# Attention, routed experts and phase mixing on one core: the shared expert slot in four column groups of 32, and a later fifth chunk

## Chip, cores and metric

One core of one Trainium2 chip runs the whole program as a single launch. The metric is device time in microseconds (us). Three runs of the kernel before gave 809.20, 811.64 and 813.08 us; their median is 811.64. The profile is one more execution.

## The reference

Three stages on `B, S, D = 4, 576, 64` with 8 heads, so 2304 tokens of 512 numbers, all in 32-bit floats:

```python
# 1. attention: scores below (row maximum - tau) are masked
scores = scale * q @ k.T
scores = where(scores >= max(scores) - tau, scores, -1e9)
x = softmax(scores) @ v                       # heads side by side: (B, S, 512)
# 2. experts: each token picks one of 8, or keeps the expert of the token before it
fresh = argmax(x @ w_gate); keep = sigmoid(x @ w_local) >= 0.5
e = previous_e if keep else fresh             # along the sequence
x = softmax(x @ w_gate)[e] * (relu(x @ w1[e]) @ w2[e])     # 512 -> 1024 -> 512
# 3. phase mixing
theta = x @ w_theta
y = w_tok_r @ (x * cos(theta)) + w_tok_i @ (x * sin(theta))
u = x + y
out = u + relu(u @ w_ch)
```

Weights of the third stage are given as 64-bit floats and are decoded on the core.

## The kernel before

**Stages.** Attention runs first, batch by batch, and the router's work in between. It writes the tokens to memory and a list that sorts them by expert. The second stage works on that list in slots of 128 tokens (single) or 256 tokens of one expert (two). A slot gathers its tokens by an indirect DMA, loads its expert's two weight matrices, multiplies, scales by the gate and scatters the rows to `scr_m`. The third stage reads `scr_m` batch by batch.

**The shared slot.** The last slot of the second stage holds tokens of two experts: 96 of one and 32 of another ("few"). Here the products are in plain 32-bit floats, and each matmul takes two passes on TensorE. The tokens are the stationary operand, the weights stream through; a matmul of some columns (tokens) writes the partitions of those tokens. So `cols` has one entry for each group of tokens with its weight tiles: tokens 0 to 63 and 64 to 95 with the first expert's, 96 to 127 with few's. For each half `z` of the 1024 hidden numbers it runs four `k` steps over the 512 inputs, then the relu on ScalarE; `turn` transposes a half of `h` for the second matrix. Then come eight `k` steps over the 1024 hidden numbers, the scaling and the scatter. The first expert's w1 lies in `w1r` and `raw`, its w2 in `w2r`; few's lie in the two tiles `stk`, w1 in the one, w2 in the other.

**Channel words.** The last matrix of the third stage, `w_ch`, comes as pairs of 32-bit words and is decoded in eight pieces beside the last slots. `more_words` issues the loads of two pieces (`stage_words`, L1486) into a ring of two buffers, so a load waits until the piece before it in that buffer has been read. `decode(n)` takes n steps of the decoding: three bit operations and a product on DVE (L1520 to L1529), a square on GpSimd (L1521); the split of a decoded piece into a high part (ScalarE, L1512) and a low one (GpSimd, L1513) comes with the first steps of the pieces behind it, or, with none left, in steps of its own.

**Order.** In these stages the instructions of TensorE, ScalarE and DVE run in the order in which the program has them (`manual_schedule(engines=MANUAL)`). SP, which issues the loads, and GpSimd are not in that list in this slot: their order is a scheduler's, with the program's order as a preference. Each engine's queue is served in order.

**Into the third stage.** `load_first_x` loads the first batch's rows, chunk by chunk of 128 tokens, before the shared slot's scatter: the slots still open have no tokens of the first batch. The fifth chunk has only 64 tokens of the first batch; its other half holds 64 tokens of the second batch, and its load (L1670) waits for the shared slot's scatter. `mix_all` (from L1560 on) is the third stage. `prep` transposes chunks (L1698), splits them in a high and a low part (L1699, L1700) and, for the chunks in `rest`, keeps a full copy (L1704). `theta(b, dh, g)` makes the angles of one half `dh` of the 512 columns for a group `g` of chunks: groups 0 and 1 have two chunks, 24 matmuls, group 2 has the fifth chunk, 12 matmuls. `wave_steps` turns angles into the products with cosine and sine: `tk` on ScalarE (L1738), four steps on DVE (L1740 to L1746), absolute value and two sines on ScalarE, products on DVE (L1752, L1754, L1761), the high parts (L1770) and the low parts `zl` and `zml` (L1779). The digits given to `wave` say which group takes its next step. `mix` (L1790 to L1792) is the token mixing: 27 matmuls a group, over all chunks, the fifth (`zmh`, `zml`) last.

The functions that the diff touches, with the line numbers of the profile:

Of the kernel before, what the change touches and what calls it, by code (L numbers as in the profile page):

```python
# [10 lines left out]
F32 = mybir.dt.float32  # L11
# [13 lines left out]
P = 128  # L25
# [7 lines left out]
SHARE = 96, 32  # L33
# [1 line left out]
STEPS = 1, 4  # L35
FAST = 117
WARM = 10
RING, SHARED_STEPS = 3, (4, 4, 10)
MANUAL = {mybir.EngineType.PE, mybir.EngineType.Activation, mybir.EngineType.DVE}
ORDERED = MANUAL | {mybir.EngineType.SP}  # L40
KH = S // 2 + D
# [13 lines left out]
class Kernel:  # L55
# [874 lines left out]
    def two_step(self, now, nxt, last, after):  # L930
        if after:
            self.load_index(after)
        few = nxt.get("few")
        for c in range(4):
            self.load_w1(nxt, c)
        if last:
            self.hidden_pair(now)
            self.hidden_out(last)
            self.pair_values(last, now)
            for _ in range(2):  # L940
                self.decode(STEPS[0] << self.halves)
        else:
            for f in range(4):
                self.hidden_two(now, f)
                if f < 3:
                    self.split_w2(now, f)
                self.decode(STEPS[0] << self.halves)
        self.more_words()
        for c in range(3):
            self.load_w2(nxt, c)  # L950
        self.tokens(nxt)
        for c in range(3):
            self.finish_two(now, c)
        if few:
            views = [[t[:, i * F:(i + 1) * F] for i in range(4)] for t in self.open_stk(F32)]
            few["w1raw"] = views[0]
            few["w2raw"] = [v.rearrange("p (t f) -> p t f", t=2) for v in views[1]]
            for c in range(4):
                self.load_w1(few, c)
        else:  # L960
            for c in range(2):
                self.split_w1(nxt, c)
        self.split_w2(now, 3)
        self.load_w2(nxt, 3)
        self.finish_two(now, 3)
        if few:
            for c in range(4):
                self.load_w2(few, c)
        else:
            for c in range(2, 4):  # L970
                self.split_w1(nxt, c)
        self.decode(STEPS[1] << self.halves)
        for h in range(2):
            self.scale(now, h, nxt["xt"][:, 1] if few else None)
            self.scatter(now, h)

    def shared_slot(self, st):
        nc = self.nc
        few, cols = st["few"], []
        for a, b, w in ((0, 64, st), (64, SHARE[0], st), (SHARE[0], P, few)):  # L980
            cols.append((slice(a, b), w.get("w1raw", self.w1raw), w.get("w2raw", self.w2raw)))
        self.more_words()
        h = self.hg.tile([P, F], F32, name="h")
        hf = self.xg.tile([P, 4, 2 * P], F32, name="xl").rearrange("p a b -> p (a b)")

        def turn(z):
            t = self.ps_x.tile([P, 4, P], F32, name="t").rearrange("p a b -> p (a b)")
            for i in range(4):
                nc.tensor.transpose(
                    t[:, i * P:(i + 1) * P], h[:, z * 512 + i * P:z * 512 + (i + 1) * P], self.ident)  # L990
            nc.scalar.activation(hf[:, z * 512:(z + 1) * 512], t, AF.Copy)
        for z in range(2):
            zs = slice(z * 512, (z + 1) * 512)
            hp = self.ps_h.tile([P, 2, 2 * P], F32, name="h").rearrange("p a b -> p (a b)")
            for k in range(4):
                for c, w1, _ in cols:
                    nc.tensor.matmul(
                        hp[c], st["xf"][:, k, c], w1[k][:, zs], start=(k == 0), stop=(k == 3), skip_group_check=True)
                if z and k == 1:
                    turn(0)  # L1000
            nc.scalar.activation(h[:, zs], hp, AF.Relu)
            self.decode(SHARED_STEPS[z])
        self.load_first_x()
        self.more_words()
        st["o"] = o = self.ps_o.tile([P, DM], F32, name="o")
        for k in range(8):
            for c, _, w2 in cols:
                nc.tensor.matmul(
                    o[c], hf[:, k * P:(k + 1) * P][:, c], w2[k // 2][:, k % 2], start=(k == 0), stop=(k == 7),
                    skip_group_check=True)  # L1010
            if k == 1:
                turn(1)
        self.decode(SHARED_STEPS[2])
        self.scale(st)
        self.scatter(st)

# [543 lines left out]
    def mix_all(self):  # L1560
# [6 lines left out]

        nc.scalar.activation(self.halfpi, self.ident[:, 0:1], AF.Sin)
        nc.vector.memset(self.halfpi, math.pi / 2)
        self.theta(0, 0, 0)  # L1570
        self.prep(0, (4,), (2,))
        for dh in range(2):
            for g in range(1 - dh, 3):
                self.theta(0, dh, g, self.ps_v if dh or g == 2 else self.ps_th)
        self.waves(0, 0)
        self.wave("01")
        self.prep(0, (), (3, 4))
        self.wave("0000" "21111" "00" "0" "2222" "11" "0" "1" "2" "1" "2" "2" "2")
        self.waves(0, 1)
        self.wave("012")  # L1580
        self.rest = []
# [108 lines left out]
    def prep(self, b, chunks, rest=()):  # L1690

        nc = self.nc
        st = self.state3[b]
        for c in chunks:
            cs = slice(c * P, (c + 1) * P)
            st["t", c] = t = self.ps_v.tile([P, 512], F32, name="v").rearrange("p (k s) -> p k s", k=4)
            for k in range(4):
                nc.tensor.transpose(t[:, k], st["x"][:, c, k * P:(k + 1) * P], self.ident)  # L1698
            nc.scalar.activation(st["xh"][:, :, cs], t, AF.Copy)  # L1699
            nc.vector.tensor_tensor(st["xl"][:, :, cs], t, st["xh"][:, :, cs].bitcast(F32), ALU.subtract)  # L1700
        for c in rest:
            n = self.chunk(c)
            for dh in range(2):
                nc.scalar.activation(  # L1704
                    st["xf", dh][:, :, c * P:c * P + n], st["t", c][:, 2 * dh:2 * dh + 2, :n], AF.Copy)
# [208 lines left out]
```

## Time and profile before

| what | value |
|---|---|
| median of three runs | 811.64 us (809.20 to 813.08) |
| the profiled execution: its time / its span | 809.36 us / 807.6 us |
| TensorE busy, weight loads busy | 773.2 us (96%), 614.3 us (76%) |
| DVE, ScalarE, GpSimd busy | 582.1 (72%), 471.9 (58%), 196.0 us (24%) |
| the shared slot's passes on TensorE | from 529.21 us on, scaled at 562.34 |
| mean DMA rate over the span | 132 GB/s |

The profile is that of one execution. Times in it count from the start of its span. PE is TensorE's matmuls, PEld its weight loads, DVE is VectorE, ACT ScalarE, POOL GpSimd, SPq the queue of DMAs that SP issues. `out<-in` are the program's names of tiles with numbers left out; L997 is a line of the kernel. A form like `128*32 128x512 f32` for a matmul is the part of the array it takes (rows by columns) and the streaming operand. An "x3" at the end of a row means that three neighbouring instructions of that line are merged in it; the duration is then from the first one's start to the last one's end. In brackets stands how long the engine was idle before, and what ended it. Matmuls are pipelined: what counts is the distance from start to start.

### The profile page before, as it was taken

The numbers are of one execution on the slowest core, as the hardware profiler recorded it, in microseconds if no ns is written. First come the engines' busy times: TensorE is split into PE (matmuls) and PEld (weight loads), VectorE is DVE, ScalarE is ACT, GpSimd is POOL, SyncE is SP. The second block draws the span as 40 slices with busy tenths as digits, with TensorE's granted clock in tenths as the row PEclk, the third lists the DMA queues.
The fourth block names the chain that finished last, engine by engine and source line by source line (L and its number), as shares of the span: only waits on it lengthen the run. The fifth ranks groups of instructions, "written<-read, shape, count | busy, mean of one in ns | idle before, by whom it ended". The sixth has DMA issues, their size and how long they took to land. (4 is left out here: it accounts for less than half of the span.)

```text
span 807.6 us, 16486 instructions
## 1 busy us (share of the span) xinstructions
PE 773.2 (96%) x6230; PEld 614.3 (76%) x6230; DVE 582.1 (72%) x1246; ACT 471.9 (58%) x941; POOL 196.0 (24%) x241
## 2 busy tenths in 40 slices
PE   7899999999999989999999999999899999999997
PEld 4455565565565578789999889932899999999997
DVE  6999999899989688568788889532695446555522
ACT  5998888887877745556555556412655335435311
POOL 4000003003002222136554455422002122033110
PEclk9999999999999999999999999999999999999999
DMA  6722323322411788789787776461010120120101
GB/s 153 183 75 81 90 75 101 115 75 76 119 48 61 261 278 213 258 329 316 262 281 244 253 241 224 159 234 54 11 53 1 46 80 1 41 72 2 59 1 59
DMA packets 67518, 106.70 MB, mean 132 GB/s; under 512 B 28194, under 2 KB 34726, under 8 KB 67432
## 3 DMA queue, kind: packets, MB, share of 16 engines
q1 hardware_dynamic: 63400, 95.33, 37.2%
q0 software_dynamic: 4032, 10.25, 3.5%
q8 instruction: 52, 0.85, 0.4%
q14 instruction: 34, 0.28, 0.1%
HBM read 94.22 MB, written 16.32 MB: 137 GB/s over the span
## 5 line engine op out<-in xcount | busy, mean ns | idle before, releaser
L332 DVE TENSOR_SCALAR_CACHE_REDUCE ns<-s,nqs 128x576 f32<-128x576 f32 x144 | 116.8, 812 | 18.6 <-PE s L313 16.6
L372 DVE SCALAR_TENSOR_TENSOR a<-ns,thr,e 128x576 f32<-128x576 f32 x144 | 117.1, 814 | 0.7 <-ACT thr L345 0.6
L338 ACT ACTIVATE e<-ns,nb 128x576 f32<-128x576 f32 x144 | 109.6, 781 | 10.3 <-DVE ns L332 10.3
L413 ACT ACTIVATE aT<-t 128x256 f32<-128x256 f32 (+1 forms) x216 | 82.6, 457 | 30.3 <-PE t L406 29.4
L313 PE MATMUL s<-raw 64*128 64x288 f32 x512 | 81.6, 427 | 9.1 <-ACT aT L399 5.0
L437 PE MATMUL o<-aT,vm 128*64 128x288 f32 x512 | 74.8, 415 | 0.0
L1304 PE MATMUL h<-xh,stk 128*128 128x256 f32 x256 | 72.9, 285 | 0.6 <-DVE hl L1293 0.6
L1305 PE MATMUL h<-xl,stk 128*128 128x256 f32 x256 | 72.4, 283 | 0.0
L1306 PE MATMUL h<-xh,stk 128*128 128x256 f32 x256 | 72.4, 283 | 0.0
L1418 DVE TENSOR_TENSOR w2l<-w2r,w2h 128x1024 fp32r<-128x1024 f32 x42 | 54.6, 1306 | 11.6 <-ACT w2h L1415 11.6
L313 PEld LDWEIGHTS s<-raw 64*128 64x128 f32 x512 | 43.5, 189 | 23.8 <-DVE ns L332 8.7
L1320 PE MATMUL o<-w2l,hh 128*128 128x512 f32 x144 | 56.4, 392 | 0.9 <-DVE w2l L1418 0.9
L437 PEld LDWEIGHTS o<-aT,vm 128*64 128x64 f32 x512 | 32.8, 136 | 32.1 <-issue 12.8
L1319 PE MATMUL o<-w2h,hh 128*128 128x512 f32 x144 | 56.9, 395 | 0.0
L1321 PE MATMUL o<-w2h,hl 128*128 128x512 f32 x144 | 56.2, 390 | 0.0
L406 PEld LDWEIGHTS t<-ident,a 64*128 64x128 f32 x1152 | 42.6, 139 | 15.4 <-ACT e L338 6.3
L406 PE MATMUL t<-ident,a 64*128 64x64 f32 x1152 | 51.6, 228 | 0.2 <-ACT aT L413 0.2
L1304 PEld LDWEIGHTS h<-xh,stk 128*128 128x128 f32 x256 | 49.1, 192 | 2.0 <-DVE hl L1293 1.7
L1415 ACT ACTIVATE w2h<-w2r 128x1024 fp32r<-128x1024 f32 x42 | 44.0, 1054 | 10.9 <-issue 7.9
L1292 ACT ACTIVATE hh<-h 128x512 fp32r<-128x512 f32 x36 | 21.3, 598 | 48.7 <-PE h L1306 43.3
L1305 PEld LDWEIGHTS h<-xl,stk 128*128 128x128 f32 x256 | 49.1, 192 | 0.5 <-issue 0.2
L1306 PEld LDWEIGHTS h<-xh,stk 128*128 128x128 f32 x256 | 49.1, 192 | 0.0
(387 smaller groups left out, 2069.2 us busy)
## 6 DMA issues: line engine op xcount, KB each, us to landing
w2r<-in_moe_w_dram SPq DMA_DIRECT2D x48, 512.0 KB, 6.5
raw<-in_moe_w_dram SPq DMA_DIRECT2D x36, 512.0 KB, 8.0
raw<-in_q_dram SPq DMA_DIRECT2D x15, 576.0 KB, 5.9
w1r<-in_moe_w_dram SPq DMA_DIRECT2D x12, 512.0 KB, 5.5
raw<-in_k_dram SPq DMA_DIRECT2D x30, 176.0 KB, 3.5
vm<-in_v_dram SPq DMA_DIRECT2D x32, 128.0 KB, 2.5
stk<-in_moe_w_dram SPq DMA_DIRECT2D x8, 512.0 KB, 7.1
out_dram<-ob SPq DMA_DIRECT2D x16, 256.0 KB, 2.2
```

Of the source, the lines that this page charges most:

```text
L313: nc.tensor.matmul(s[:, z, :SH], qd[rows, int(j != z), cs], kd[rows, j * KH:j * KH + SH], start=True, stop=True)
L332: nc.vector.tensor_scalar(ns, s[:, :, :SH], self.nqs[:, 0:1], None, ALU.mult, ALU.min, accum_out=nb)
L338: self.nc.scalar.activation(e, pr["s", c, j], AF.Exp, bias=pr["nb", c][:, j:j + 1], scale=-1.0)
L372: nc.vector.scalar_tensor_tensor(a.rearrange("p (z s) -> p z s", z=2), s, thr, e, ALU.is_le, ALU.mult, accum_out=total)
L406: nc.tensor.transpose(t[h][:, 4 * n + b], a[r, (k + b) * P:(k + b + 1) * P], self.ident[r, r])
L413: nc.scalar.activation(self.pairs[i]["aT"][:, b:b + w, s0:s0 + D], t[h][:, 4 * n:4 * n + w], AF.Copy)
L437: self.last_av = nc.tensor.matmul(o[j * D:(j + 1) * D, :SH], vm[:, j, c - 1, :], aT[:, 4 * j + c - 1, zs], start=(z == 0 and c == 1), stop ...
L1304: nc.tensor.matmul(h[:, i], wh[:, fs], xh, start=(k == 0), stop=False)
L1305: nc.tensor.matmul(h[:, i], wh[:, fs], xl, start=False, stop=False)
L1306: nc.tensor.matmul(h[:, i], wl[:, fs], xh, start=False, stop=(k == 3))
L1319: nc.tensor.matmul(o, hh, wh[:, i], start=(q == i == 0), stop=False)
L1320: nc.tensor.matmul(o, hh, wl[:, i], start=False, stop=False)
```

## The change

The shared slot's tokens are cut into four groups of 32, each with the weight tiles of its expert: three of the first expert and one of few. The loads of few's w2 move from the slot before into the shared slot, behind its first `more_words`. The decoding steps move ahead of each half's relu, eight in each half; the second `more_words` moves from behind `load_first_x` to behind the first half's relu, and after the second matrix the decoding runs until nothing is left. In the third stage the fifth chunk is transposed behind the first two groups of angles of the first half, and the first steps of their waves; the angles of that chunk come after the first group of the other half. The buffer of the fifth chunk's transposes is taken from its pool ahead of the others' angles.

```diff
--- before.py
+++ after.py
@@ -35,7 +35,7 @@
 STEPS = 1, 4
 FAST = 117
 WARM = 10
-RING, SHARED_STEPS = 3, (4, 4, 10)
+RING, SHARED_STEPS = 3, (8, 8)
 MANUAL = {mybir.EngineType.PE, mybir.EngineType.Activation, mybir.EngineType.DVE}
 ORDERED = MANUAL | {mybir.EngineType.SP}
 KH = S // 2 + D
@@ -963,10 +963,7 @@
         self.split_w2(now, 3)
         self.load_w2(nxt, 3)
         self.finish_two(now, 3)
-        if few:
-            for c in range(4):
-                self.load_w2(few, c)
-        else:
+        if not few:
             for c in range(2, 4):
                 self.split_w1(nxt, c)
         self.decode(STEPS[1] << self.halves)
@@ -977,9 +974,12 @@
     def shared_slot(self, st):
         nc = self.nc
         few, cols = st["few"], []
-        for a, b, w in ((0, 64, st), (64, SHARE[0], st), (SHARE[0], P, few)):
-            cols.append((slice(a, b), w.get("w1raw", self.w1raw), w.get("w2raw", self.w2raw)))
+        for a in range(0, P, 32):
+            w = st if a < SHARE[0] else few
+            cols.append((slice(a, a + 32), w.get("w1raw", self.w1raw), w.get("w2raw", self.w2raw)))
         self.more_words()
+        for c in range(4):
+            self.load_w2(few, c)
         h = self.hg.tile([P, F], F32, name="h")
         hf = self.xg.tile([P, 4, 2 * P], F32, name="xl").rearrange("p a b -> p (a b)")
 
@@ -998,10 +998,11 @@
                         hp[c], st["xf"][:, k, c], w1[k][:, zs], start=(k == 0), stop=(k == 3), skip_group_check=True)
                 if z and k == 1:
                     turn(0)
+            self.decode(SHARED_STEPS[z])
             nc.scalar.activation(h[:, zs], hp, AF.Relu)
-            self.decode(SHARED_STEPS[z])
+            if z == 0:
+                self.more_words()
         self.load_first_x()
-        self.more_words()
         st["o"] = o = self.ps_o.tile([P, DM], F32, name="o")
         for k in range(8):
             for c, _, w2 in cols:
@@ -1010,7 +1011,8 @@
                     skip_group_check=True)
             if k == 1:
                 turn(1)
-        self.decode(SHARED_STEPS[2])
+        while self.active or self.last:
+            self.decode(1)
         self.scale(st)
         self.scatter(st)
 
@@ -1567,15 +1569,19 @@
 
         nc.scalar.activation(self.halfpi, self.ident[:, 0:1], AF.Sin)
         nc.vector.memset(self.halfpi, math.pi / 2)
+        self.state3[0]["t", 4] = self.ps_v.tile([P, 512], F32, name="v").rearrange("p (k s) -> p k s", k=4)
         self.theta(0, 0, 0)
-        self.prep(0, (4,), (2,))
-        for dh in range(2):
-            for g in range(1 - dh, 3):
-                self.theta(0, dh, g, self.ps_v if dh or g == 2 else self.ps_th)
+        self.theta(0, 0, 1)
+        self.prep(0, (), (2,))
         self.waves(0, 0)
-        self.wave("01")
-        self.prep(0, (), (3, 4))
-        self.wave("0000" "21111" "00" "0" "2222" "11" "0" "1" "2" "1" "2" "2" "2")
+        self.wave("01" "000")
+        self.prep(0, (4,), (3,))
+        self.theta(0, 1, 0, self.ps_v)
+        self.theta(0, 0, 2, self.ps_v)
+        self.theta(0, 1, 1, self.ps_v)
+        self.prep(0, (), (4,))
+        self.theta(0, 1, 2, self.ps_v)
+        self.wave("0" "21111" "00" "0" "2222" "11" "0" "1" "2" "1" "2" "2" "2")
         self.waves(0, 1)
         self.wave("012")
         self.rest = []
@@ -1693,7 +1699,9 @@
         st = self.state3[b]
         for c in chunks:
             cs = slice(c * P, (c + 1) * P)
-            st["t", c] = t = self.ps_v.tile([P, 512], F32, name="v").rearrange("p (k s) -> p k s", k=4)
+            if ("t", c) not in st:
+                st["t", c] = self.ps_v.tile([P, 512], F32, name="v").rearrange("p (k s) -> p k s", k=4)
+            t = st["t", c]
             for k in range(4):
                 nc.tensor.transpose(t[:, k], st["x"][:, c, k * P:(k + 1) * P], self.ident)
             nc.scalar.activation(st["xh"][:, :, cs], t, AF.Copy)
```

## Rows read from the trace of the kernel before

**Rows 1.** the page: busy time of each engine; the chain that ended last
```profile
PE 773.2 (96%) x6230; PEld 614.3 (76%) x6230; DVE 582.1 (72%) x1246; ACT 471.9 (58%) x941; POOL 196.0 (24%) x241
...
PE 28%; DMA 1%; DVE 0%; ACT 0%; issue 0%; SPq 0%; POOLq 0%; ACTq 0%
```

**Rows 2.** the chain of waits in order of time: start us, us, what
```profile
563.30 4.91 DMA scr_m<-raw,idx
...
571.83 0.21 PE th L1719
```

**Rows 3.** TensorE's timeline behind the slot: start us, us, line, names, [idle before]
```profile
567.79 0.28 PE L1721 MATMUL th<-th,xTl 128*128 128x256 f32 x1
570.99 0.84 PE L1698 MATMUL v<-ident,raw 128*128 128x128 f32 x4 [2.92 <-DMA raw<-scr_m]
```

**Rows 4.** windows: stretch, us, busy of PE, PEld, DVE, ACT, POOL, clock, DMA
```profile
526.00:534.00 8.00, 8.00 (x29) 3.25 (x27) 1.39 (x5) 1.38 (x2) 1.96 (x2) 1.00 0.98 343
571.00:574.80 3.80, 3.80 (x20) 3.80 (x21) 1.81 (x3) 1.73 (x4) 0.46 (x1) 0.55 0.00 0
584.30:600.00 15.70, 15.66 (x118) 15.44 (x118) 15.03 (x33) 9.42 (x20) 0.00 (x0) 1.00 0.18 62
```

**Rows 5.** TensorE's timeline in the shared slot: first step, start of second half
```profile
529.21 1.62 PE L997 MATMUL h<-w1r,xh 128*64 128x512 f32 x3
530.22 0.62 PE L997 MATMUL h<-stk,xh 128*32 128x512 f32 x1
...
530.67 0.59 PE L997 MATMUL h<-stk,xh 128*32 128x512 f32 x1
531.20 1.62 PE L997 MATMUL h<-raw,xh 128*64 128x512 f32 x3
...
545.68 1.62 PE L1008 MATMUL o<-w2r,xl 128*64 128x512 f32 x3
```

**Rows 6.** TensorE's timeline at the router's matmuls: first passes, second passes, next line
```profile
82.40 0.45 PE L470 MATMUL g<-xT,wg 128*32 128x288 f32 x4
...
82.66 0.43 PE L470 MATMUL g<-xT,wg 128*32 128x288 f32 x4
...
83.02 0.72 PE L406 MATMUL t<-ident,a 64*128 64x64 f32 x16
```

**Rows 7.** timelines of SP's queue, VectorE and ScalarE in the shared slot
```profile
523.83 2.10 SPq L1257 DMA_DIRECT2D stk<-in_moe_w_dram  x4
526.45 1.07 SPq L1486 DMA_DIRECT2D w<-in_moe_w_ch_dram  x2
537.11 7.52 SPq L1687 DMA_DIRECT2D raw<-scr_m  x5
...
536.30 0.29 DVE L1520 TENSOR_SCALAR val<-w 128x256 int32<-128x256 int32 x1 [8.91 <-DMA w<-in_moe_w_ch_dram]
539.04 0.80 DVE L1520 TENSOR_SCALAR val<-w 128x256 int32<-128x256 int32 x1 [2.44 <-POOL ch L1513]
...
541.94 0.75 DVE L1529 SCALAR_TENSOR_TENSOR val<-ch,val 128x256 f32<-128x256 f32 x2
...
529.32 0.69 ACT L1398 ACTIVATE xt<-o,idx 128x512 f32<-128x512 f32 x1 [0.67 <-PE o L1321]
537.29 0.60 ACT L1001 ACTIVATE h<-h 128x512 f32<-128x512 f32 x1 [7.29 <-PE h L997]
...
562.34 0.69 ACT L1398 ACTIVATE raw<-o,idx 128x512 f32<-128x512 f32 x1 [6.16 <-PEq L833]
```

**Rows 8.** timelines of VectorE and TensorE from the angles to token mixing
```profile
572.50 0.69 DVE L1700 TENSOR_TENSOR xTl<-v,xTh 128x512 fp32r<-128x512 f32 x1 [3.70 <-ACT xTh L1699]
...
575.53 0.43 DVE L1746 TENSOR_SCALAR tr<-tr 128x512 f32<-128x512 f32 x1
576.75 0.43 DVE L1740 TENSOR_SCALAR tk<-tk 128x512 f32<-128x512 f32 x1 [0.79 <-ACT tk L1738]
...
588.00 0.40 PE L1792 MATMUL y<-wt,zml 128*128 128x288 f32 x1
```

## Prediction

> **What bounds the kernel now.** I read the page first, then the chain of waits, then the timeline of each engine over the two stretches that the diff touches. TensorE is busy for 96% of the span, and the chain that ended last has nearly nothing but TensorE in it [rows 1]. So a microsecond counts if TensorE is spared it, or if it stood idle in it. Two such places lie in the diff's reach. In the shared slot TensorE issues matmul passes from 529.21 to about 562.2 us without a gap, so that stretch is bound by how these passes share the array. Behind it the chain leaves TensorE for a scatter (563.30) and a load [rows 2]: TensorE ends a group of angles at about 568.0, stands idle until the fifth chunk's data lets its transposes start at 570.99 [rows 3], and after that idle time its granted clock is 0.55 of 2.4 GHz from 571.0 to 574.8, most of it at the lower level of 1.2 GHz [rows 4]. All times below are on the span's own axis.
>
> **Four column groups.** A step (one k) of the slot has a matmul of 64 columns and two of 32, each in two passes. The 64 columns start at 529.21, the 32-column pair at 530.22, its second passes at 530.67, and the next step at 531.20 [rows 5]: 1.01 + 0.45 + 0.53 = 1.99 us. The pair of 32s already runs side by side, one with the weights of one expert and one with the other's: what they cost together, 0.98, is about what the 64 columns cost alone. The change puts all 128 columns into four groups of 32, so I expect one round of two passes for a step. That four groups run side by side is shown in this kernel by the router's matmuls: four of 128x32 by 288 elements start within one row (82.40), their second passes at 82.66, and the next line's work at 83.02 [rows 6]. That is 0.26 from pass to pass; for 512 elements 0.26 x 512/288 = 0.46. With 0.92 a step the sum is 16 steps x (1.99 - 0.92) = **17.1 us saved**. Bounds: 0.98 a step, as a pair has it now with its 0.53 tail (16.2 saved), and twice the 0.45 between a pair's passes, 0.90 (17.4 saved). I take 0.92 as the only row with four groups gives it.
>
> A passage of the Trainium skill bears on the difference between 0.92 and 0.98: TensorEngine Tiling (Array Packing), "Key Properties", says that a change of the tiling mode drains the engine. The 0.53 in rows 5 lies where the shape changes from 32 columns to 64, the 0.45 inside a shape, and in rows 6 the change of shape takes 0.36 where a pass takes 0.26; so the rows agree. By that rule no step but those beside the transposes pays the drain and 0.92 holds; without it 0.98 would.
>
> The number of matmuls goes from 3 to 4 a step, 128 passes where there were 96; their issue is hidden as long as four groups leave no gap, as in rows 6. The two turns of h stay as they are. The slot's last pass should then end at 562.2 - 17.1 = 545.1, and its second half begin at about 537.2 (545.68 before [rows 5], 16.47 after the start: eight steps and a turn).
>
> **What must arrive earlier for it.** (a) The four w2 loads of the second expert move behind the channel words on SP's program. Today they are issued from 523.83 to 525.9, the words from 526.45 [rows 7], right after the DVE has read the two words before. If SP takes the new order, the w2 loads stand behind that wait and go out from 527.5, 3.7 us later. They are 2.1 MB; at the rate of that stretch, 343 GB/s [rows 4], they take 6 us, so they land by about 536.5, the first of them near 532, and TensorE needs them one by one, 1.84 us apart, from 537.2. I cost this at nothing; the cover is some 5 us, and what goes beyond it stands as idle TensorE, one for one. (b) The words then land near 529.5 and not at 536.30. Their decoding takes 6.4 us today (536.30 to 541.94 + 0.75), 2.44 of it waiting until GpSimd has freed a buffer, which hung on ScalarE's split behind the first relu at 537.29 [rows 7]. In the new order of ScalarE the split stands ahead of that relu, behind the scaling at 529.32, so it runs at 530.0. The last pair of words is asked for at about 535, and decoded by 542, before the slot's end. Nothing of the DVE's or GpSimd's decoding is on TensorE's path; ScalarE's split is, if it waits: behind it are queued the relu, then the turn on TensorE. (c) The first batch's rows: their five loads wait today for the scatters before them until 537.11 [rows 7]; that does not move, the last is issued by 540 and lands by 543, and TensorE wants them at 546. They are also behind the last words' two issues on SP if SP keeps program order, which costs nothing, since these go out before 537. Price if (c)'s cover is gone: the amount by which the loads are late, at most 1 or 2 us.
>
> **The fifth chunk behind two groups of angles.** The chain from the slot's end (scale at 562.34, scatter at 563.30, data at 570.99) keeps its length [rows 2, 3, 7]. In it TensorE now does 16 transposes and one group of angles (24 matmuls), then waits 2.92. In the slow stretch the matmuls of a group take 0.21 each [rows 2]; at the full clock that is 0.21 x 0.55 = 0.12, so a second group of 24 takes 2.9: it fills the wait, and the transposes come when the data does. With the wait the slow clock goes, in which about 15 matmuls took 0.09 more each, 1.4. On TensorE alone that is 4.3 us. But the angles must pass ScalarE and DVE before token mixing can use them, and there the DVE is next: the last matmul of the first mixing group waited for its last product, zml, until 588.00 [rows 8], and the DVE is busy 15.03 of the 15.7 us from 584.3 to 600 [rows 4], so nothing is regained there. What moves is therefore the DVE's chain. In the new order tk and three steps of the first group (some 1.8 us of DVE) go ahead of the fifth chunk, into idle time that lasts until 572.50. Then comes the chunk's low part, which still needs its data, at 572.5 to 573.2 as now, and then the clip of the first group, at 573.2 and not at 575.53 (2.3 earlier). Today the DVE then waits 0.79 for the second group's tk, until 576.75 [rows 8]; that group's angles are now done at 570.9, so its first step follows the clip at 573.65: **3.1 us earlier**. From there both orders have the same DVE work with no gaps. So TensorE gains 3.1 of its 4.3, and the rest stays as short waits for zl and zml in the first mixing group. Bounds: 0 (another engine holds the chain) and 4.3.
>
> **Sum.** 17.1 + 3.1 = 20.2. The profiled execution took 809.36 us (span 807.6 and 1.76 around it): 809.4 - 20.2 = 789.2. The median of the three runs shown, 811.64, lies 2.3 above that execution, and the new time will be such a median: 791.4, so I say **791.5**.
>
> **Rivals.**
> 1. *Words late.* SP may still put the w2 loads ahead of the words: in this slot SP's order is not written out by hand, and the loads are ready sooner. Then the words land at 536.30 as now, the second half's relu stands on ScalarE behind splits that wait for the decode (536.3 + 6.4 - 2.4 = 540.3, with the splits about 540.7), and ends at 541.3, where TensorE asks for it at 539.0: 2.4 us of idle TensorE, 793.8. For it speaks that today's order is just that; against it, only that the program's order is now the other. Chance 0.25.
> 2. *Four groups cost more than two.* Each group brings its own stream of 512 elements, where rows 6 have 288. If the second pair overlaps with the first by half only, a step lies midway between 0.98 and 1.96, at 1.47; the slot saves 16 x 0.52 = 8.3, and with 3.1 the time is 800.2. The even start of four streams in rows 6 speaks against it. Chance 0.07. The Trainium skill has a milder case of this: TensorE: Matmul & The Clock Gate, "Measured speedup vs the span model", gives a speedup of 3.07 and not 4 for four tiles (by rows), which would be 4 x 0.98 / 3.07 = 1.28 a step and, as an estimate, 797.1; no run here shows it for 512 elements.
> 3. *Angles gain nothing*, since the DVE or the late data holds the first mixing group as long as before: 811.6 - 17.1 = 794.5. Against it speaks the 0.79 of idle DVE at 576.75 and the 3.7 before 572.50. Chance 0.05.
> 4. *Groups run two by two*: 1.96 a step, 16 x 0.03 + 3.1 = 3.6 saved, 808.0. Chance 0.03.
> 5. *Slower: the groups run one after another*, since with other weights streaming they find one port. Then a step has four times 0.98, 3.92, the slot grows by 16 x 1.93 = 30.9, and with 3.1 back the time is 839.4. It decides from 2.18 a step on (1.99 + 3.1/16). Against it: the pair in rows 5 has the two experts' weights side by side already, and rows 6 have four streams. Chance 0.03.
>
> The forecast has 0.55, and 0.02 is left for what I do not see.
>
> **Range.** About 0.5% (4 us) is what a measurement of this kernel can tell from no change. My case with its bounds spans 811.6 - 17.4 - 4.3 = 789.9 to 811.6 - 16.2 - 2.3 = 793.1, where 2.3 is the clip's part of the shift alone; the three runs shown scatter by about 2 to either side. With rivals 1 and 3, and that scatter on both ends, the range is **788 to 798**; rivals 2, 4 and 5 and the unknown stay outside. Faster: the forecast, rivals 1 to 3 and part of the rest, 0.93. Same: rival 4, 0.03. Slower: rival 5 and part of the unknown, 0.04.
>
> **What the new trace would show.** Right: steps of the slot 0.92 apart with eight passes of 128x32 each, and the slot some 16 us long; the words' first DVE step near 530; the fifth chunk's transposes right behind the second group of angles, granted clock 1.00 there; zml 3 us nearer to the slot's end. Wrong: steps of 1.2 or more; an idle TensorE ahead of the slot's second turn, put down to the relu; a wait for w2 at the second half; a wait for the fifth chunk that is still there.

## The result, and the profile after

| | us |
|---|---|
| before: median of 4 runs | 811.67 (809.20 to 813.08) |
| changed: median of 4 runs | **789.77** (788.34 to 790.73) |
| ratio | 0.9732, 95% interval 0.9702 to 0.9762 |
| profiled executions | 809.36 to 790.73 |
| their spans | 807.6 to 789.0 |

The forecast was 791.5, in a range from 788 to 798. The interval of the ratio means 19.3 to 24.2 us saved.

The page of the changed kernel, the busy times and the shares of the chain that answer to [rows 1]:

```profile
PE 757.2 (96%) x6262; PEld 614.0 (78%) x6262; DVE 585.9 (74%) x1246; ACT 472.0 (60%) x941; POOL 188.0 (24%) x241
...
PE 29%; DVE 1%; ACT 0%; issue 0%; DVEq 0%; ACTq 0%
```

TensorE is busy 16 us less, with 32 more matmuls; the DMA is gone from the end chain.

TensorE's timeline of the changed kernel, from the slot's first step to the first transposes behind it; it answers to [rows 3, 5]:

```profile
530.94 0.63 PE L997 MATMUL h<-w1r,xh 128*32 128x512 f32 x3
530.96 0.62 PE L997 MATMUL h<-stk,xh 128*32 128x512 f32 x1
531.39 0.60 PE L997 MATMUL h<-w1r,xh 128*32 128x512 f32 x3
...
531.82 0.61 PE L997 MATMUL h<-raw,xh 128*32 128x512 f32 x3
...
538.55 0.61 PE L1009 MATMUL o<-w2r,xl 128*32 128x512 f32 x3
...
545.73 0.59 PE L1009 MATMUL o<-stk,xl 128*32 128x512 f32 x1
548.16 1.94 PE L1706 MATMUL v<-ident,raw 128*128 128x128 f32 x16 [1.84 <-PEq L833]
```

Four groups start within 0.02 us, two of them with different experts' weights; the second passes follow after 0.45, the next step at 531.82. The second half begins 7.61 behind the first step, where it was 16.47. The passes take 15.38 us (530.94 to 546.32) instead of 33.0. But TensorE then stands idle for 1.84 us, put down to its own sequencer at L833; in the kernel before it was 0.86 (transposes at 563.08), put down to ScalarE's at the same line:

```profile
563.08 1.97 PE L1698 MATMUL v<-ident,raw 128*128 128x128 f32 x16 [0.86 <-ACTq L833]
```

L833 is the branch at run time that skips the slots for leftover tokens. Every engine has a compare-and-branch and, behind it, semaphore instructions there; the latter are called the meeting below.

SP's queue, ScalarE and VectorE of the changed kernel, which answer to [rows 7]; L1488 issues the channel words, L1259 the second expert's w2, L1676 the fifth chunk:

```profile
528.18 0.81 SPq L1488 DMA_DIRECT2D w<-in_moe_w_ch_dram  x2
529.19 2.10 SPq L1259 DMA_DIRECT2D stk<-in_moe_w_dram  x4
536.67 0.87 SPq L1488 DMA_DIRECT2D w<-in_moe_w_ch_dram  x2
...
552.70 0.46 SPq L1676 DMA_DIRECT2D raw<-scr_m  x1
...
545.78 0.75 ACT L1514 ACTIVATE ch<-val 128x256 fp32r<-128x256 f32 x2 [4.11 <-DVE val L1531]
546.47 0.69 ACT L1400 ACTIVATE raw<-o,idx 128x512 f32<-128x512 f32 x1
...
541.66 0.74 DVE L1522 TENSOR_SCALAR val<-w 128x256 int32<-128x256 int32 x1 [4.05 <-DMA w<-in_moe_w_ch_dram]
```

The words go out ahead of w2, as in the program. The last pair of words reaches the DVE at 541.66, and ScalarE's last split ends just before the scale of the slot's result, 0.15 behind the last pass (0.12 before): the cover is used up, but it holds. This execution is the tightest. In experiments 3, 5 and 9, with the same slot, ScalarE is done with its splits and idle for 1.4 to 1.5 us before the scale; here the last piece of words reached the DVE 1.7 us behind the piece before it (543.34 against 541.66).

The end of the chain, on TensorE, DVE and in windows of the changed kernel; it answers to [rows 4, 8]. The columns of the windows are the stretch, its length, busy time of PE, PEld, DVE, ACT and POOL, the granted clock, the DMA share and GB/s:

```profile
555.80 0.60 PE L1706 MATMUL v<-ident,raw 128*128 128x128 f32 x4
...
569.38 0.40 PE L1800 MATMUL y<-wt,zml 128*128 128x288 f32 x1
...
557.21 0.69 DVE L1708 TENSOR_TENSOR xTl<-v,xTh 128x512 fp32r<-128x512 f32 x1 [0.54 <-ACT xTh L1707]
557.82 0.42 DVE L1754 TENSOR_SCALAR tr<-tr 128x512 f32<-128x512 f32 x1
558.15 0.69 DVE L1748 TENSOR_SCALAR tk<-tk 128x512 f32<-128x512 f32 x1
...
555.70:558.00 2.30, 2.30 (x22) 2.30 (x21) 1.73 (x4) 1.79 (x5) 0.01 (x1) 1.00 0.00 0
```

The fifth chunk is transposed without a wait and at clock 1.00, and the second group's first step follows the first group's clip (557.82) at once.

**The account.** From the first slot pass to the matmul that takes zml the kernel before needs 588.00 - 529.21 = 58.79 us, the changed one 569.38 - 530.94 = 38.44, so 20.35 less: 17.63 in the passes, 0.98 lost in the idle time behind them, 3.70 between the first transposes and that matmul (24.92 to 21.22). Behind it both spans have 219.6 us left. Ahead of it this execution of the changed kernel was 1.73 us later, in work that the diff doesn't touch; in the executions below that start lies anywhere from 529.25 to 535.32. That is spread between executions, and so the spans differ by 18.6.

### The profile page after: what moved, and what is told of

Same layout as the page of the kernel before. It is cut to its first block, busy times and chain, and to the rows that moved or that the text cites. A ratio compares the mean times of both kernels' runs of the same rounds, so it can differ in the third digit from the quotient of the medians.

```text
span 789.0 us, 16551 instructions
## 1 busy us (share of the span) xinstructions
PE 757.2 (96%) x6262; PEld 614.0 (78%) x6262; DVE 585.9 (74%) x1246; ACT 472.0 (60%) x941; POOL 188.0 (24%) x241
## 5 line engine op out<-in xcount | busy, mean ns | idle before, releaser
L437 PE MATMUL o<-aT,vm 128*64 128x288 f32 x512 | 76.4, 422 | 0.0
```

The costliest lines, as they stand in the source:

```text
L437: self.last_av = nc.tensor.matmul(o[j * D:(j + 1) * D, :SH], vm[:, j, c - 1, :], aT[:, 4 * j + c - 1, zs], start=(z == 0 and c == 1), stop ...
```

## The experiments

Experiments 1 to 4, 5 to 8, and 9 and 10 each ran on one chip, beside runs of the kernel before there (medians 810.74, 813.88, 810.80 us). Ratios are to these, and times of two kernels are compared only inside such a set.

**1. Without the four groups.** The changed kernel, with the old shapes:

```diff
-        for a in range(0, P, 32):
-            w = st if a < SHARE[0] else few
-            cols.append((slice(a, a + 32), ...
+        for a, b, w in ((0, 64, st), (64, SHARE[0], st), (SHARE[0], P, few)):
+            cols.append((slice(a, b), ...
```

> The changed kernel with the shared slot's columns cut as before (64, 32 and 32), all else as changed. Theory: nearly the whole gain of the slot is the shape of the groups, 0.86 us a step with four groups of 32 against 1.99 with 64 + 32 + 32. Then the slot grows by 16 x 1.13 = 18.1 us; the 1.0 us that TensorE now idles longer behind the slot, until GpSimd's last split of channel words is done, goes, since that split is then long done. About 789.8 + 17.1 = 807, ratio to before 0.993 to 0.997. Rival: the order of loads and decoding gives part of the slot's gain; then the slot is shorter than 33 us even with three groups and the time is under 803.

Measured: 808.95 us (805.86 to 810.82, 10 runs), ratio 0.9976, 0.9951 to 1.0001. Its transposes on TensorE:

```profile
566.10 1.97 PE L1705 MATMUL v<-ident,raw 128*128 128x128 f32 x16 [0.86 <-ACTq L833]
```

The passes take 33.01 us again (from 532.23), and the idle time is back at 0.86 with ScalarE. So the slot's gain, and the new idle time with it, hang on the four groups; the order of the loads gains nothing while the passes are long. The expectation put that idle time down to GpSimd's last split; TensorE's row names the branch at L833, and without the branch 0.86 is left (experiment 9). The trace keeps the opening's gain (21.26 to zml's matmul in the table below); the time shows 1.9 us, with an interval from 0 to 4.0, and the ratio lies just above the 0.993 to 0.997 expected.

**2. The four groups alone.** The kernel before, with only that loop changed.

> The kernel before with four groups of 32 as the only edit; loads, decoding steps and the third stage as before. Theory: the passes take 15.4 us and not 33, but the loads and the decoding, which stood beside 33 us, don't fit: the last two pieces of channel words are asked for behind the first batch's rows, land some 8 us after the second half begins, and their decoding and GpSimd's split (7 to 8 us from landing) end some 6 us after TensorE's last pass. All engines meet behind the slot, so TensorE idles there for 6 to 7 us more: saved 17.6 - 6.5 = 11, about 800.5 us, ratio 0.984 to 0.989, with an idle TensorE behind the slot. Rival: decoding is off the path, as the kernel before has it, and 17 us or more are saved, 794 or less.

Measured: 796.70 us (795.54 to 801.17, 5 runs), ratio 0.9836, 0.9808 to 0.9864. TensorE's timeline and one window:

```profile
550.38 2.83 PE L1699 MATMUL v<-ident,raw 128*128 128x128 f32 x16 [3.80 <-ACTq L833]
...
558.48 0.64 PE L1699 MATMUL v<-ident,raw 128*128 128x128 f32 x4 [1.70 <-DMA raw<-scr_m]
...
550.00:557.00 7.00, 6.39 (x40) 6.19 (x40) 2.78 (x6) 5.09 (x11) 1.91 (x3) 0.76 0.08 30
```

The passes take 15.39 us, so the shape alone makes the slot's gain. With the old order of the loads the last words reach the DVE at 545.83, ScalarE's split waits for it until 549.00, and the scale queued behind that split starts at 549.66. TensorE waits 3.80 us in place of 1.84, then runs at a mean clock of 0.76. My expectation put the delay at GpSimd's part of the decoding; TensorE went on while GpSimd was still at it, so that step was wrong, and the saving larger than expected for it.

**3. Without the new opening of the third stage.** The changed kernel, with the old `mix_all`:

```diff
         self.theta(0, 0, 0)
-        self.theta(0, 0, 1)
-        self.prep(0, (), (2,))
+        self.prep(0, (4,), (2,))
+        for dh in range(2):
+            for g in range(1 - dh, 3):
+                self.theta(0, dh, g, self.ps_v if dh or g == 2 else self.ps_th)
...
```

> The changed kernel with the third stage's opening as before: the fifth chunk transposed behind one group of angles, the waves behind it. Theory: the wait for the fifth chunk (2.9 us) and the slow clock behind it come back, VectorE's chain to zml starts later, and 3.7 us are lost: about 793.5 us, ratio to before 0.977 to 0.979, zml 24.4 us after the first transposes and not 20.7. Rival A: VectorE's chain is not what holds it and the whole 4.3 us of TensorE are lost, 794.1. Rival B: the later order gains nothing and the time stays at 789.8.

Measured: 792.07 us (790.40 to 794.84, 5 runs), ratio 0.9764, 0.9738 to 0.9790. TensorE's timeline and one window:

```profile
549.64 1.94 PE L1702 MATMUL v<-ident,raw 128*128 128x128 f32 x16 [2.09 <-PEq L833]
...
556.62 0.63 PE L1702 MATMUL v<-ident,raw 128*128 128x128 f32 x4 [2.02 <-DMA raw<-scr_m]
572.33 0.40 PE L1796 MATMUL y<-wt,zml 128*128 128x288 f32 x1
...
556.60:560.40 3.80, 3.78 (x33) 3.80 (x33) 1.98 (x4) 2.00 (x5) 0.46 (x1) 1.00 0.00 0
```

From transposes to zml's matmul it takes 22.69, so the opening is worth 1.5 here, not the 3.7 of the account. The wait for the fifth chunk is 2.02 and not 2.92, since the scatter (548.65) left 0.99 ahead of the first transposes and not 0.2 behind them, and the clock stays at 1.00. Beside experiment 2 this shows what the new order of loads and decoding steps, taken together, is worth once the slot is short: 796.70 - 792.07 = 4.6 us, with intervals that don't meet. In the two traces it is 2.8 (43.00 against 40.17 in the table below).

**4. Two groups of 64.** The changed kernel; tokens 64 to 95 get the other expert's products:

```diff
-        for a in range(0, P, 32):
-            w = st if a < SHARE[0] else few
+        for a in range(0, P, 64):
+            w = st if a < 64 else few
```

> The changed kernel with two groups of 64 columns in the slot, 0 to 63 with the first expert's weights, 64 to 127 with the other's; tokens 64 to 95 so get the other expert's products (left out: their own). Theory: what counts is that all groups of a step have one shape and run together, not that they are narrow: two passes a step at 0.43, 0.86 us a step, the slot 15.4 us. Rival: groups of 64 columns run one after the other as the 64-column matmul stood alone before (1.01 each), so 2.0 us a step and a slot of 33 us; a third way, that each pass of 64 costs 0.5 where one of 32 costs 0.43, gives 1.0 a step and 17.6 us.

One run: 790.26 us. TensorE's timeline, and SP's part of the meeting at L833 (columns there: instruction, count, duration in ns, first and last start):

```profile
529.25 0.64 PE L997 MATMUL h<-w1r,xh 128*64 128x512 f32 x1
529.26 0.64 PE L997 MATMUL h<-stk,xh 128*64 128x512 f32 x1
529.74 0.59 PE L997 MATMUL h<-w1r,xh 128*64 128x512 f32 x1
...
547.69 1.94 PE L1706 MATMUL v<-ident,raw 128*128 128x128 f32 x16 [3.01 <-SPq L833]
...
L833 SPq EVENT_SEMAPHORE  x9: 17/17/17, 546.8 to 547.4; - x9
```

The pair of 64s runs side by side, at the same 0.43 a pass, and the passes take 15.43 us. Narrow groups are not what saves; groups of one shape that fill the array together are. The old split paid for having 64 beside 32. Here TensorE read its branch at 540.2 and had it done before its last pass, and the idle time ended with SP's part of the meeting at L833. GpSimd's scatter in that trace (546.59, 1.91 behind the last pass) is put down to the DMA of the first rows; that SP waited for the same is likely, not shown.

**5. The changed kernel again**, unchanged, as the base of 6 to 8:

> The changed kernel once more, beside the runs below. Theory: ratio to before 0.973, as in its first runs; TensorE idle 1.8 us behind the slot, because its branch behind the slot takes 3.9 us from the moment the sequencer reads it, and that is only 2.7 us ahead of TensorE's last pass (5.0 us in the kernel before). The old opening of the third stage gave 0.9764 on this measure; so its new opening is worth some 1.5 to 2.5 us, 0.2 to 0.3%. Rival: this profile has another cause for the 1.8 us, and they vary from run to run by more than 0.3.

Measured: 795.66 us (792.95 to 802.40, 6 runs), ratio 0.9770, 0.9727 to 0.9814. TensorE's transposes, the window on them, and its branch:

```profile
553.28 3.56 PE L1706 MATMUL v<-ident,raw 128*128 128x128 f32 x16 [2.58 <-PEq L833]
...
553.20:557.00 3.80, 3.72 (x19) 3.75 (x20) 1.64 (x3) 2.08 (x5) 0.00 (x0) 0.55 0.17 58
...
L833 PEldq COMPARE_BRANCH  x1: 4679/4679/4679, 548.0 to 548.0; - x1
```

The idle time is 2.58 and not 1.84, as the branch takes 4.68 and not 3.94; and this time the clock falls to 0.55 behind it, which makes the stretch up to zml's matmul 22.66 and not 21.22. So the rival is half right: the cause is the same, but the idle time varies by more than 0.3. And against the 0.9764 of experiment 3 this ratio shows no gain of the new opening in the changed kernel.

**6. Three DVE steps of the first group behind the fifth chunk** (same set):

```diff
-        self.wave("01" "000")
+        self.wave("01")
...
-        self.wave("0" "21111" ...
+        self.wave("0000" "21111" ...
```

> The changed kernel with the three VectorE steps of the first group taken behind the fifth chunk's transposes and not ahead of them; TensorE's order is as changed. Theory (VectorE's chain sets the first mixing group): the fifth chunk's low part runs at the same time, the three steps (1.81 us) follow it, the 0.54 us that VectorE waits today ahead of that low part stays idle, and zml comes 1.8 us later; TensorE waits that much longer in the first mixing group; the time grows by 1.8 us (0.23%). Rival (TensorE's filled wait is what the new opening gains): TensorE does its angles at the same times and zml comes no later.

Measured: 797.16 us (794.44 to 801.81, 6 runs), ratio 0.9788, 0.9749 to 0.9826. TensorE's timeline:

```profile
550.98 3.24 PE L1706 MATMUL v<-ident,raw 128*128 128x128 f32 x16 [2.57 <-DMA w<-in_moe_w_ch_dram]
...
571.23 0.40 PE L1800 MATMUL y<-wt,zrl 128*128 128x288 f32 x1 [1.67 <-DVE zrl L1787]
...
576.06 0.30 PE L1800 MATMUL y<-wt,zml 128*128 128x288 f32 x1
```

The clock behind the idle time was 0.56, as in experiment 5, so the two compare. DVE makes zml at 574.80, 23.82 behind the first transposes, where experiment 5 has 22.18: 1.6 more, near the 1.8 expected, and TensorE waits 1.67 for zrl. Its matmul with zml comes 2.42 later (25.08 against 22.66): behind that wait the clock is 0.50, the lower level, from 571.9 to 575.2. So the three steps in the DVE's idle time are worth 1.6, as much as the whole opening in the changed kernel (1.5 in experiment 3), and nearly half of its 3.7 beside the old slot. The times (1.5 apart) have intervals that overlap.

**7. The slot's last four steps in two groups of 64** (same set; tokens 64 to 95 get the other expert's products there), to have TensorE read the branch sooner:

```diff
-            for c, _, w2 in cols:
+            for c, _, w2 in cols if k < 4 else wide:
```

> The changed kernel with the last four steps of the slot's second matrix in two groups of 64 columns and not four of 32 (8 instructions of TensorE a step and not 16); tokens 64 to 95 then get the other expert's second matrix in those steps (left out: their own). Theory (the branch): the passes keep their pace, 0.43, the slot ends as before, but TensorE's sequencer gets to the branch behind the slot some 1.7 us sooner ahead of the last pass, so it waits for ScalarE's scaling alone: 0.9 to 1.0 us of idle TensorE behind the slot and not 1.84. Rival (the loads of the first rows or GpSimd's last split hold the meeting point): still 1.8 us or more.

Measured: 796.98 us (796.46 to 798.41, 4 runs), ratio 0.9784, 0.9743 to 0.9826. TensorE's timeline:

```profile
551.05 1.07 PE L1708 MATMUL v<-ident,raw 128*128 128x128 f32 x8 [1.89 <-PEq L833]
553.97 1.53 PE L1708 MATMUL v<-ident,raw 128*128 128x128 f32 x8 [1.86 <-issue]
```

The branch was read 3.7 us ahead of the last pass's end (545.5 against 549.16), where experiment 5 has 2.7, but it took 4.84, and the idle time was 1.89, not 0.9 to 1.0. SP's part came at 550.4 too, so the run doesn't tell which held. What made the second gap of 1.86 is open; behind it the clock is 0.57 (554.0 to 557.0).

**8. The new opening alone** (same set): the kernel before with the new `mix_all`.

> The kernel before with the third stage's new opening as the only edit. Theory: there the wait for the fifth chunk (2.92 us) is followed by the slow clock, which also delays the second group's angles; both go. From the first transposes to the matmul that takes zml it took 24.9 us; now 21.2 to 21.8, so 3.1 to 3.7 us are saved, ratio 0.9955 (about 807.2 us). Rival: as with the changed slot, where old and new opening differ by 1.5 us from transposes to zml: 809, 0.998.

Measured: 810.46 us (808.99 to 812.04, 12 runs), ratio 0.9955, 0.9936 to 0.9974, as expected. TensorE's timeline:

```profile
566.35 1.97 PE L1704 MATMUL v<-ident,raw 128*128 128x128 f32 x16 [0.86 <-ACTq L833]
...
587.59 0.40 PE L1798 MATMUL y<-wt,zml 128*128 128x288 f32 x1
```

From transposes to zml's matmul it takes 21.24 in place of 24.92: 3.7 us saved, which is what the ratio shows (2.1 to 5.2).

**9 and 10. Without the branch.** The changed kernel and the kernel before, each with this taken out:

```diff
-            with tc.If(self.total > 0):
-                with ExitStack() as nest:
-                    ...
-                self.load_first_x()
```

> The kernel after the change, without the run-time branch behind the shared slot and its body (the slots for leftover tokens, which these inputs do not fill, and the second load of the first rows behind them). It leaves out what the kernel would need for other inputs. Theory (TensorE's own branch, read only 2.7 us before its last pass because a step is now 0.86 us long, stands in the open): without it TensorE goes on as soon as the first rows are there; these landed 0.0 to 0.6 us behind the last pass in the trace after the change, so the idle time behind the slot falls from 1.84 (2.58 in the repeat) to at most 0.9, put down to a load or to nothing, and the time falls by 1 to 2 us: ratio to before 0.970 to 0.972. Rival (the loads of the first rows end the idle time, the branch only stands beside them): the idle time stays at 1.5 to 2.6, now put down to the DMA of the first rows, ratio 0.973 to 0.976.

Measured: 789.77 us (789.49 to 791.58, 5 runs), ratio 0.9746, 0.9722 to 0.9770. TensorE's timeline and SP's load of the fifth chunk:

```profile
547.18 1.97 PE L1697 MATMUL v<-ident,raw 128*128 128x128 f32 x16 [0.86 <-ACT raw L1391]
...
568.43 0.40 PE L1791 MATMUL y<-wt,zml 128*128 128x288 f32 x1
...
550.08 0.45 SPq L1667 DMA_DIRECT2D raw<-scr_m  x1
```

> The kernel before the change, without the same branch and body (left out as in changed_no_branch). Theory (in the kernel before, the branch lay under the slot's passes, 1.6 us to spare, and only ScalarE's part of the meeting stood in the open): the 0.86 us behind the slot fall to 0.0 to 0.5, the time falls by 0.3 to 0.9 us, ratio 0.9985 to 1.000, too little to tell in time but plain in the trace. So the branch's removal is worth about 1 us more after the change than before it. Rival (the meeting costs as much before as after, and the difference of 1.84 and 0.86 is scatter): both kernels gain the same within 0.3 us in the idle time behind the slot.

Measured: 805.91 us (804.07 to 812.19, 12 runs), ratio 0.9954, 0.9932 to 0.9975. The same rows of this kernel:

```profile
563.10 1.97 PE L1689 MATMUL v<-ident,raw 128*128 128x128 f32 x16 [0.84 <-ACT raw L1389]
568.53 0.63 PE L1689 MATMUL v<-ident,raw 128*128 128x128 f32 x4 [0.45 <-ACT halfpi L1559]
...
565.99 0.46 SPq L1661 DMA_DIRECT2D raw<-scr_m  x1
```

In the idle time behind the slot the difference is as expected: the branch costs the changed kernel 1.84 - 0.86 = 0.98 us, the kernel before nothing (0.86 to 0.84, where I expected 0.0 to 0.5). What is left, 0.86, is put down to ScalarE's scale of the slot's result. The edit takes out the meeting with the branch; that TensorE's branch was the part that held is read from the rows: in the changed kernel SP's part ends at 546.9, ScalarE's at 547.2, TensorE's at 547.6. As a time the 1 us can't be seen, and the ratio is above the 0.970 to 0.972 expected.

But the kernel before gains 3.7 us by the ratio where I expected 0.3 to 0.9. It gains them in the opening (563.10 to zml's matmul at 584.23: 21.13, not 24.92), just what the new opening gains. The rows of the branch at L833, first in the kernel before, show where (PEldq is the sequencer of TensorE's weight loads), and below them stands SP's load of the fifth chunk:

```profile
L833 PEldq COMPARE_BRANCH  x1: 3338/3338/3338, 557.2 to 557.2; - x1
...
L833 POOLq INC_SWDGE_SEM  x1: 1460/1460/1460, 566.8 to 566.8; - x1
...
568.46 0.46 SPq L1670 DMA_DIRECT2D raw<-scr_m  x1
```

and in the changed one:

```profile
L833 SPq EVENT_SEMAPHORE  x9: 17/17/17, 546.2 to 546.9; - x9
L833 PEldq COMPARE_BRANCH  x1: 3939/3939/3939, 543.6 to 543.6; - x1
L833 PEldq EVENT_SEMAPHORE  x1: 51/51/51, 547.6 to 547.6; - x1
L833 POOLq INC_SWDGE_SEM  x1: 1460/1460/1460, 551.0 to 551.0; - x1
```

GpSimd issues the slot's scatter, passes the branch, and then has 1.46 us of bookkeeping of its DMA semaphores, which ends at 568.26 before and 552.46 after; the fifth chunk's load, which waits for that scatter, is issued 0.2 behind it in both (568.46, 552.70), and about 0.2 behind it in the other eight traces with the branch. So from scatter to load it takes 5.16 and 4.86 us with the branch, and 2.67 (563.32 to 565.99) and 2.7 without. Without the branch the data comes in time for the old order too, and the new opening has nothing left to gain: 21.13 us from transposes to zml's matmul with the old one, 21.25 with the new.

All kernels on one footing, from their TensorE rows: the slot's first pass, the length of its passes, the idle time behind, first transposes to zml's matmul, and the sum. Behind zml's matmul every span has 219.5 to 219.7 us left.

| kernel | first pass | passes | idle | to zml | sum |
|---|---|---|---|---|---|
| before | 529.21 | 33.01 | 0.86 | 24.92 | 58.79 |
| changed | 530.94 | 15.38 | 1.84 | 21.22 | 38.44 |
| 1 three_groups | 532.23 | 33.01 | 0.86 | 21.26 | 55.13 |
| 2 groups_alone | 531.19 | 15.39 | 3.80 | 23.81 | 43.00 |
| 3 old_mixing | 532.16 | 15.39 | 2.09 | 22.69 | 40.17 |
| 4 two_by_64 | 529.25 | 15.43 | 3.01 | 21.21 | 39.65 |
| 5 changed_again | 535.32 | 15.38 | 2.58 | 22.66 | 40.62 |
| 6 waves_behind | 533.02 | 15.39 | 2.57 | 25.08 | 43.04 |
| 7 wide_ends | 533.62 | 15.54 | 1.89 | 24.66 | 42.09 |
| 8 opening_alone | 532.49 | 33.00 | 0.86 | 21.24 | 55.10 |
| 9 changed_no_branch | 530.93 | 15.39 | 0.86 | 21.25 | 37.50 |
| 10 before_no_branch | 529.26 | 33.00 | 0.84 | 21.13 | 54.97 |

## Why the prediction was right, point by point

- **What bounds the slot: right.** The passes did, and nothing took their place. Experiment 2 saves 17.6 us in the passes with the shape alone, experiment 1 loses them again.
- **The price of a step: 0.92 was a little high.** It is 0.86 to 0.88, below the lower bound of 0.90: 17.6 saved where the sum had 17.1. The bounds came from groups of unlike shape or shorter operands; the steady stream of like groups here is faster than both. Rivals 2, 4 and 5 fall with it (1.47, 1.96, 3.92 a step). The Trainium skill's speedup of 3.07 for four tiles by rows (TensorE: Matmul & The Clock Gate, "Measured speedup vs the span model") gave 1.28 a step as an estimate; the trace says 0.86, and the measurement decides. The Trainium skill's rule that a change of the tiling mode drains the engine (TensorEngine Tiling (Array Packing), "Key Properties") agrees with the passes of 0.43 where the shape stays, against 0.53 [rows 5] where it changed, and 0.55 ahead of a turn of h in the changed kernel (535.68 to 536.23).
- **The order of the loads at nothing: right, with less cover than I said.** SP kept the program's order, so rival 1 fell. I had the last words decoded by 542, some 3 us ahead of the last pass. The last two DVE steps on them run from 545.34 to 546.09, which is 544.4 with the slot's start moved back to 529.21, and only 0.2 ahead of the last pass; in experiments 3, 5 and 9 it is 1.7 to 1.9. The first rows I had landed by 543, 3 us ahead of TensorE. In experiments 4 and 6 GpSimd's scatter is put down to their DMA, 1.9 and 1.7 us behind the last pass, so there that cover was gone. Without the new order of loads and decoding, experiment 2 against 3, the short slot would have cost 4.6 us more (2.8 in the traces): rival 1 (2.4) had the right kind of danger and put it at the second half's relu; the runs show it at the last scale.
- **What is late next behind the slot: missed.** I wrote of the loads and ScalarE there, not of the branch. TensorE reads it ahead of its queued matmuls; that was 5.0 us ahead of the last pass's end before (557.2 against 562.2), and is 2.7 now (543.6 against 546.3), while a step has 16 instructions in 0.86 us where it had 12 in 1.99. What sets how far ahead it reads is open: about 15 matmuls were still to start then, and about 20 now. The branch takes 3.3 to 4.8 us in the ten traces that have it, so it now ends after the passes: 0.98 us lost in this execution, against experiment 9. It isn't always what ends last: with the short slot and the branch the idle time was 1.84 to 3.01 us (3.80 with the old loads), and in experiments 4 and 6 SP's part of the meeting ended behind TensorE's.
- **The opening: 3.7, not 3.1, by the steps named.** Counted from the first transposes, the chunk's low part starts at 9.05 (9.42 before), the clip at 9.66 (12.45) and the second group's first step at 9.99 (13.67 [rows 8]): the DVE chain is 3.68 earlier. The forecast had the low part where it was, which is 0.37 of the 0.6 too little; the rest is that I added the durations of two steps (0.7 and 0.45) where they start 0.61 and 0.33 apart. Rival 3 falls (experiment 8). But the cause that I gave for the old wait was incomplete: I took the 7.7 us from scatter to data as fixed; 2.5 of them go with the branch (experiment 10), and the rows put them at GpSimd's passage through it.
- **The sum.** 17.6 - 1.0 + 3.7 = 20.35 against 20.2: two small terms too low and one missed, which cancel; that they come within 0.15 is luck. The terms don't simply add, either: beside the old slot the opening is worth 3.7 (experiment 8), beside the new one 1.5 (experiment 3 against the changed kernel), since TensorE comes later behind the scatter there and the clock stays at 1.00. The median's 21.9 has both sums in its interval. The 2.3 that I added because the median lay above the profiled execution did not come back: the new median lies 0.96 below its profiled execution, and 1.7 below the forecast.

## What to carry to other kernels

When matmuls of some columns share the array, cut them into groups of one shape that fill it together; here 64 + 32 + 32 cost 1.99 a step, and 32 four times or 64 twice 0.86. When a stretch on the busiest engine is halved, look at once for what lay hidden beneath it by its length alone: here the decoding (3.8 us of idle time, and not 1.8, if its loads aren't moved) and a branch at run time. And a wait for a DMA is worth following to what its semaphore passes through: reordering work into the wait and removing its cause bought the same 3.7 us, once.

## What the runs showed of the hardware

- The branch at run time is dear on TensorE alone: 3.34 to 4.84 us in ten traces from when its sequencer reads it, 0.05 to 0.07 on the other engines. In these 4 us the changed kernel's DMA has five packets on its two instruction queues, the kernel before has one in its 3.3 us. The Trainium skill (Runtime: NRT & Kernel Launch, "Instruction fetch mechanics") says that a taken branch to a target outside the fetched window waits for a DMA of that page. The packets don't speak against it; no run here shows that they are the cause.
- The clock behind an idle time doesn't follow its length: 1.00 behind 1.84, 2.02, 2.09 and 3.01 us (changed kernel, experiments 3 and 4), and 0.50 to 0.57 of 2.4 GHz, all or most of it at the lower level of 1.2, behind 1.67, 1.86, 2.57, 2.58 and 2.92 us (experiments 6, 7, 6, 5, and the kernel before). In experiments 5 and 6, where it fell ahead of them, the first 16 transposes took 3.2 to 3.6 us and not 1.94. So two executions of one kernel can differ: experiment 5 has 1.4 us more up to zml's matmul than the first trace.
